# Column sums of w_out in another PSUM bank, its loads ordered ahead, and two pairs with unsplit attention weights

## The chip, the cores and the metric

One of the eight cores of a Trainium2 chip runs the whole program. The metric is the device time of one execution in microseconds; the kernel before takes 1210.42 us (median of three runs, 1209.32 to 1211.03). A core has five engines that each work through their own list of instructions in order and wait for each other by semaphores: PE (TensorE, matrix products, with PEld for its weight loads), DVE (VectorE), ACT (ScalarE), POOL (GpSimd) and SP (SyncE, which here issues every DMA). Matrix products land in PSUM, eight banks of 128 x 512 float32 values.

## The reference

Attention with a sigmoid in place of a softmax, followed by a two-layer feed-forward net with an ELU between the layers. Eight batches, twelve heads, 448 positions, head size 64; model width 768, hidden width 2048. `moe_w_in` and `moe_w_out` are float64.

```python
scores = scale * np.matmul(q, k.transpose(0, 1, 3, 2)) - np.log(S)
attn = 1.0 / (1.0 + np.exp(-scores))
x = np.matmul(attn, v)                  # (8, 12, 448, 64) -> 3584 tokens x 768
h = x @ w_in                            # 768 -> 2048
g = np.where(h > 0.0, h, np.exp(np.minimum(h, 0.0)) - 1.0)
out = g @ w_out                         # 2048 -> 768
```

## The kernel before

**Numbers in two halves.** To keep precision at float16 speed, a float32 operand is scaled by a power of two and split into a high and a low float16 part (`split`: ACT writes the high part, DVE the low one from it). A product of two split operands is three matmuls: high x high, low x high, high x low. The scales come from the largest value of an operand, or, for the two weights, from the sum of magnitudes down a column.

**Order of the work.** The heads of a batch go in six pairs. Batch 0 (`b < EXACT`) is done with unsplit float32 operands: scores, sigmoid, then values against the float32 attention weights, while the tiles of `w_in` are loaded, decoded from float64 and split beside it. Then `hidden(0, w_out_beside)` runs the first layer of batch 0 (`moe1`, sixteen tiles `ph` of 18 matmuls), with the work on `w_out` beside it. From batch 1 on, each batch's six pairs are interleaved with the second layer (`moe2`, tiles `po`) of the batch ahead, and its own first layer follows.

**w_out.** `load_w_out` takes its two column halves i = 0 and 1, each in sixteen row tiles f. For each tile there is a load of 384 KB, two ACT passes (`magnitudes`, L154 and L158), a DVE pass (L159), one matmul of the magnitudes against ones into the PSUM tile `so` (L166), and a DVE pass that puts the sign back (`signed`, L173). When all sixteen are summed, `sum_magnitude` (L180 to L182) makes the scale, and sixteen splits (L137 on ACT, L138 on DVE) write the two halves into `wo`. The split of tile f writes over the place of magnitudes f-2, so ACT's split waits for DVE's split two tiles back. The generator is advanced by `step`: four pieces per `ph` tile from the third on, and what is left in the first pairs of batch 1 (`step(3 if hp < NC - 1 else NF)`). The raw tiles have no buffers of their own: they lie in parts of `wo` that are not yet written (eight places for half 0, two for half 1) or in the three buffers with the tag "at", so a load waits for `signed` of the tile whose place it takes.

**PSUM.** Three buffers have the tag "pm" (the `ph` and `po` tiles, small sums, and `so`), two of two banks have "psc" (scores), one has "pav" (a pair's sum over values; `ph` tile 3 of each batch also uses it).

**A pair from batch 1 on.** `prepare` finds the scales (DVE's `mx`, a matmul `pr`, small DVE and POOL steps), splits q and k (`nat`), sends them through a transposing DMA into `qk`, and splits the values into `vn`. `Pair.scores` makes three score tiles `psc0` to `psc2` of two heads, and one (`pscr`) for the last keys of two pairs; `soften` is the sigmoid on ACT (L400, into `sg`); `Pair.parts` splits `sg` into `at` (L436 on ACT, L437 on DVE) and the last keys into `ar` (L425, L427); `Pair.values` multiplies these by `vn` into `pav`; `finish` splits `pav` into `xh`.

**What sets the order.** Up to the end of batch 0's first layer a scheduler places each engine's instructions, DMAs on SP among them; the loop over batches 1 to 7 stands in the order in which it is written (`manual_schedule`), and leftovers of the first part are merged between its instructions. So a change in the first part can move any instruction there.

Of the kernel before, what the change touches and what calls it, by code (L numbers as in the profile page):

```python
# [34 lines left out]
def attention_ffn(  # L35
# [22 lines left out]
    WR, WT = 5, 5  # L58
    EXACT = 1
    SP = 4  # L60
    SKEW = 2
    W_IN = [1, 3, 6, 9, 12, 15, 16]
    W_LOAD = [1, 1]
    W_OUT = 4
    assert 2 * D == P and 2 * R == P and NK == NP

# [151 lines left out]
    def load_w_out(wo):  # L218


        for i in range(NH):
# [5 lines left out]
            ]  # L227
            sums = ps.tile([P, 512], F32, tag="pm", name=f"so{i}", bufs=3)
            for f in range(NF):

                if i == 0 and f >= 2:
                    st = wo[:, 1, f % 8 * 2 :][:, :2]
                elif i == 1 and f % 2 and f < NF - SP - SKEW:
                    st = wo[:, 1, NF - SP + f // 2 % 2 * 2 :][:, :2]
                else:
                    st = None
# [7 lines left out]
                )  # L244
                lo, hi, hl = words(st)
                t = whole[f].unsqueeze(1)
# [30 lines left out]

    def load_v(b, hp):
        rv = rvs[(b * NP + hp) % len(rvs)]
        both = slice(2 * hp, 2 * hp + 2)  # L280
# [10 lines left out]
    def value_scale(b, hp, pv, c, xs):  # L291
# [7 lines left out]
        nc.vector.reciprocal(vi[:, hp : hp + 1], vm[:, hp : hp + 1])  # L299
        if b < EXACT:  # L300
            nc.gpsimd.tensor_scalar(c, vi[:, hp : hp + 1], 2.0 ** (XTOP - XBITS), None, op0=ALU.mult)
# [6 lines left out]
    def prepare(b, hp, raw, rv, xs):  # L308
# [34 lines left out]
        def transposed(sc):  # L343
# [23 lines left out]
            parts = [qk[:, i].rearrange("p t x -> p (t x)") for i in range(2)]  # L367

            vn = sb.tile([P, 2, 2 * NC + 2, D], F16, tag="vn", name=f"vn{u}", bufs=3)
            split(vn[:, 0], vn[:, 1], rv, sc[:, 0:1])  # L370
# [4 lines left out]
    class Pair:  # L375
# [42 lines left out]
        def parts(self, g):  # L418

            if g == NC:  # L420
                (sg, i) = self.sg[g]
# [20 lines left out]
        def values(self, g):  # L442
            if g == 0:
                self.pav = ps.tile([P, 512], F32, tag="pav", name=f"pav{self.u}")
            pav, sg, vv = self.pav, self.sg.pop(g), self.vs
            if g == NC and self.b < EXACT:
                for j, r in enumerate(rows):
                    nc.tensor.matmul(
                        pav[r, :S], vv[0][r, 2 * NC + j], sg[0][r, 0], start=False, stop=True
                    )  # L450
# [78 lines left out]
    def moe1(b, g, xh, m, first, beside=None):  # L529
# [8 lines left out]
        for f in range(NF):  # L538

            if f == 3:  # L540
                ph = ps.tile([P, 512], F32, tag="pav", name=f"ph{b}_{f}")
# [126 lines left out]
    def w_out_beside(f):  # L668
        nonlocal wo, steps
        if f == 0:  # L670
            w_in_ratios()
            wo = sb.tile([P, NH, NF, 2, HM], F16, tag="wo", name="wo")
            steps = load_w_out(wo)
        if f >= 2:
            step(W_OUT)
# [172 lines left out]
```

## Time and profile before

| | before |
|---|---|
| median of three runs | 1210.42 us |
| profiled execution | 1210.77 us |
| span of its instructions | 1209.0 us |
| PE busy | 1153.2 us (95%) |
| DVE busy | 827.7 us (68%) |
| ACT busy | 719.3 us (59%) |
| POOL busy | 103.0 us (9%) |
| granted PE clock over the span | 0.982 |
| read from and written to memory | 59.77 MB and 11.01 MB |

The span is counted from the first to the last instruction; the execution's own time is 1.8 us longer. The shares are means over stages with different limits, so a stage has to be read by itself. "Idle before" in a row is the time for which the engine stood just before that instruction, with the instruction or transfer that ended it.

### The profile page before, as it was taken

The page shows a single profiled execution, that of the slowest core. Times are in us where ns is not written, and L with a number is a line of the kernel's source. Part 1 is how long each engine was busy: PE and PEld are TensorE (multiplying, and loading weights), DVE is VectorE, ACT ScalarE, POOL GpSimd, SP SyncE. Part 2 cuts the span into 40 slices and gives each one's busy share as a digit, 9 for nine tenths or more (in the row PEclk, how much of TensorE's full clock was granted, in tenths as well). Part 3 has the DMA queues.
Part 4 walks back from the last instruction along what each step waited for, and adds up shares of the span by engine and source line. Part 5 has one row for each costly group of instructions (what it writes and reads, how often), then busy time and mean ns, then how long its engine had stood idle before and what let it go on. Part 6 is the DMA issues. An engine that isn't in the chain of part 4 may idle for free.

```text
span 1209.0 us, 24046 instructions
## 1 busy us (share of the span) xinstructions
PE 1153.2 (95%) x9674; PEld 639.0 (53%) x9674; DVE 827.7 (68%) x1742; ACT 719.3 (59%) x1099; POOL 103.0 (9%) x275
## 2 busy tenths in 40 slices
PE   6879785999999999999999999999999999999998
PEld 2324343555566555655566555655566555555565
DVE  5797888977667675977667666886667666865500
ACT  4875788864666446864666446864566446863300
POOL 1021001200011000200011000200011000100000
PEclk9999897999999999999999999999999999999999
DMA  8955632441124212441124212441124211310000
GB/s 224 279 145 117 210 104 74 93 99 40 40 60 93 60 40 47 93 100 40 40 60 93 60 40 47 85 107 40 40 54 99 60 40 40 76 29 8 1 27 27
DMA packets 219568, 91.62 MB, mean 76 GB/s; under 512 B 183616, under 2 KB 215360, under 8 KB 219456
## 3 DMA queue, kind: packets, MB, share of 16 engines
q1 hardware_dynamic: 219456, 90.09, 30.9%
q8 instruction: 75, 1.23, 0.4%
q14 instruction: 37, 0.30, 0.1%
HBM read 59.77 MB, written 11.01 MB: 59 GB/s over the span
## 4 chain that ended last, share of the span: by engine, by line
PE 83%; DVE 6%; ACT 4%; DMA 3%; SPq 2%; issue 1%; POOL 0%; DVEq 0%; ACTq 0%
PE ph L549 32%; PE po L581 30%; PE pav L459 7%; PE psc L392 7%; PE po_r L581 5%; PE pscr L479 1%; DMA stage<-in_moe_w_in_dram 1%; SPq L269 1%; DMA wo<-in_moe_w_out_dram 1%; DVE mx L141 1%; DVE wo L138 1%; DVE stage L159 1%; ACT wo L154 1%; DVE wi L138 1%; ACT wo L158 0%
## 5 line engine op out<-in xcount | busy, mean ns | idle before, releaser
L549 PE MATMUL ph<-xh,wi 128*128 128x448 f16 x2304 | 446.9, 356 | 12.7 <-DVE xh L500 5.1
L581 PE MATMUL po<-wo,g 128*64 128x384 f16 (+1 forms) x4320 | 395.0, 329 | 1.9 <-DVE alw L180 1.7
L581 PEld LDWEIGHTS <-g 128*64 128x64 f16 (+1 forms) x4992 | 290.8, 109 | 164.3 <-issue 33.1
L549 PEld LDWEIGHTS <-wi 128*128 128x128 f16 x2304 | 225.1, 99 | 230.2 <-issue 22.3
L437 DVE SCALAR_TENSOR_TENSOR at<-sg,at 128x896 f16<-128x896 f32 x126 | 134.0, 1090 | 91.5 <-ACT at L436 91.3
L561 ACT ACTIVATE e<-ph,msc 128x448 f32<-128x448 f32 x128 | 80.9, 633 | 185.7 <-PE ph L549 160.7
L400 ACT ACTIVATE sg<-psc,bias,sc 128x896 f32<-128x896 f32 x126 | 133.8, 1094 | 3.8 <-PE psc L392 0.5
L563 DVE TENSOR_SCALAR e<-e 128x448 f32<-128x448 f32 x128 | 50.2, 393 | 117.3 <-ACT e L561 117.2
L436 ACT ACTIVATE at<-sg 128x896 f16<-128x896 f32 x126 | 114.9, 947 | 0.7
L137 ACT ACTIVATE g<-e,msc 128x384 f16<-128x384 f32 (+1 forms) x192 | 96.2, 533 | 9.9 <-DVE e L564 8.5
L137 ACT ACTIVATE xh<-pav,sc 128x448 f16<-128x448 f32 x48 | 30.4, 633 | 116.3 <-PE pav L459 114.8
L138 DVE SCALAR_TENSOR_TENSOR g<-e,msc,g 128x384 f16<-128x384 f32 (+1 forms) x192 | 94.7, 522 | 2.4 <-ACT g L137 1.9
L392 PE MATMUL psc<-qk 64*128 64x448 f16 x756 | 87.2, 353 | 4.8 <-ACT sg L400 4.8
L564 DVE SCALAR_TENSOR_TENSOR e<-ph,msc,e 128x448 f32<-128x448 f32 x128 | 87.4, 683 | 4.1
L459 PE MATMUL pav<-at,vn 128*64 128x448 f16 x756 | 79.3, 355 | 0.0
L459 PEld LDWEIGHTS <-vn 128*64 128x64 f16 x924 | 53.1, 111 | 33.0
L137 ACT ACTIVATE nat<-raw,sc 128x384 f16<-128x384 f32 (+1 forms) x126 | 60.9, 535 | 13.5 <-POOL sc L334 9.1
L336 POOL TENSOR_SCALAR sc<-pw 128x1 f32<-128x1 f32 x42 | 12.0, 286 | 640.8 <-DVE pw L103 537.5
L581 PE MATMUL po_r<-wo,g 128*64 128x384 f16 (+1 forms) x672 | 64.9, 326 | 0.0
L138 DVE SCALAR_TENSOR_TENSOR nat<-raw,sc,nat 128x384 f16<-128x384 f32 (+1 forms) x126 | 60.8, 526 | 3.4 <-ACT nat L137 1.1
L392 PEld LDWEIGHTS <-qk 64*128 64x128 f16 x756 | 30.2, 94 | 53.4 <-issue 34.6
L589 DVE TENSOR_SCALAR o<-po,osc 128x384 f32<-128x384 f32 x48 | 29.4, 612 | 41.1 <-PE po L581 36.4
(108 smaller groups left out, 936.7 us busy)
## 6 DMA issues: line engine op xcount, KB each, us to landing
stage<-in_moe_w_in_dram SPq DMA_DIRECT2D x16, 768.0 KB, 6.3
raw<-in_q_dram SPq DMA_DIRECT2D x96, 96.0 KB, 3.3
raw<-in_k_dram SPq DMA_DIRECT2D x96, 96.0 KB, 2.8
rv<-in_v_dram SPq DMA_DIRECT2D x48, 192.0 KB, 2.8
out_dram<-o SPq DMA_DIRECT2D x48, 192.0 KB, 2.1
wo<-in_moe_w_out_dram SPq DMA_DIRECT2D x19, 384.0 KB, 4.1
so<-in_moe_w_out_dram SPq DMA_DIRECT2D x13, 384.0 KB, 4.1
rv<-in_v_dram SPq DMA_DIRECT2D x96, 32.0 KB, 2.5
```

What stands on the lines that cost most here:

```text
L137: nc.scalar.mul(hi, src, s)
L138: nc.vector.scalar_tensor_tensor(lo, src, s, hi, op0=ALU.mult, op1=ALU.subtract)
L392: nc.tensor.matmul(psc[:, j, :S] if g < NC else psc[rows[j], 0, :S], kk[rows[j], o], qq[rows[j], :S], start=(n == 0), stop=(n == len(parts ...
L400: a = nc.scalar.activation(to, psc, AF.Sigmoid, bias=bias, scale=self.s_scale)
L436: nc.scalar.mul(hi, sg, 2.0**ATOP)
L437: nc.vector.scalar_tensor_tensor(lo, sg, 2.0**ATOP, hi, op0=ALU.mult, op1=ALU.subtract)
L459: nc.tensor.matmul(pav[rows[j], :S], vv[i][:, 2 * NC + j if g == NC else j * NC + g], sg[k][:, j], start=(g == 0 and n == 0), stop=(g == N ...
L549: nc.tensor.matmul(ph[:, :S], wi[:, wj, c, f * P : (f + 1) * P], xh[:, c, xj], start=(n == 0), stop=(n == 3 * NK - 1),)
L561: a = nc.scalar.activation(e, ph[:, :S], AF.Exp, scale=inv)
L563: nc.vector.tensor_scalar(e, e, 1.0, -1.0, op0=ALU.min, op1=ALU.add)
L564: nc.vector.scalar_tensor_tensor(e, ph[:, :S], inv, e, op0=ALU.mult, op1=ALU.max)
L581: nc.tensor.matmul(po[r, :HM], tokens[:, r], wo[:, i, f, wj], start=(n == 0), stop=(n == 3 * NF - 1),)
```

## The change

1. The sums of `w_out` (`so`) take the PSUM buffer "pav" in place of one of the three "pm" buffers. In batch 0's first layer, tile 3 no longer takes "pav".
2. `load_w_out` issues its loads ahead of their use: six tiles ahead for half 0 and two for half 1 (`W_AHEAD`), and its first piece is stepped at f = 0 (`step(1)`).
3. For the first two pairs of batch 1 (`WHOLE = EXACT * NP + 2`), `parts` returns at once: the attention weights stay in `sg` as float32, the values are loaded a second time as float32 into `vw` (one load of 192 KB and two of 32 KB for a pair) in place of the split into `vn`, and `values` multiplies the two unsplit. The scale of the result follows in `value_scale`.

```diff
+    WHOLE = EXACT * NP + 2
...
+    W_AHEAD = [6, 2]
...
-            sums = ps.tile([P, 512], F32, tag="pm", name=f"so{i}", bufs=3)
-            for f in range(NF):
-
+            sums = ps.tile([P, 512], F32, tag="pav", name=f"so{i}")
+            loads = []
+
+            def load(f):
+                if f >= NF:
+                    return
                 if i == 0 and f >= 2:
                     st = wo[:, 1, f % 8 * 2 :][:, :2]
                 elif i == 1 and f % 2 and f < NF - SP - SKEW:
...
+                loads.append(st)
+
+            early = W_AHEAD[i]
+            for f in range(early):
+                load(f)
+            for f in range(NF):
+                load(f + early)
+                lo, hi, hl = words(loads[f])
                 t = whole[f].unsqueeze(1)
                 magnitudes(t, lo, hi, hl, sums[:, :HM], f == 0, f == NF - 1)
...
-    def load_v(b, hp):
-        rv = rvs[(b * NP + hp) % len(rvs)]
+    def load_v(b, hp, rv=None):
+        if rv is None:
+            rv = rvs[(b * NP + hp) % len(rvs)]
...
-        if b < EXACT:
+        if b * NP + hp < WHOLE:
             nc.gpsimd.tensor_scalar(c, vi[:, hp : hp + 1], 2.0 ** (XTOP - XBITS), None, op0=ALU.mult)
...
+            if b * NP + hp < WHOLE:
+                whole = sb.tile([P, 2 * NC + 2, D], F32, tag="vn", name=f"vw{u}", bufs=3)
+                return x_scale, s_scale, parts, [load_v(b, hp, whole)]
...
         def parts(self, g):
 
+            if len(self.vs) == 1:
+                return
...
-            if g == NC and self.b < EXACT:
-                for j, r in enumerate(rows):
+            if g == NC and len(vv) == 1:
+                i = sg[1] if len(sg) > 1 else 0
+                for j in range(2):
+                    r = rows[j ^ i]
                     nc.tensor.matmul(
-                        pav[r, :S], vv[0][r, 2 * NC + j], sg[0][r, 0], start=False, stop=True
+                        pav[rows[j], :S], vv[0][r, 2 * NC + j], sg[0][r, i],
+                        start=False, stop=True,
                     )
                 return
...
-            if f == 3:
+            if f == 3 and b >= EXACT:
                 ph = ps.tile([P, 512], F32, tag="pav", name=f"ph{b}_{f}")
...
             steps = load_w_out(wo)
+            step(1)
```

Three places show how instructions move; line numbers of the changed kernel are those of its own text (L159 is L161 there, L173 is L175, L138 is L140, L242 is L247, L437 is gone for these pairs).

DVE, from the last sums of w_out's half 1 to the splits that follow them, before (`so_13` to `so_15` are raw tiles, `at_0` the split weights of pair 0 of batch 1, `nat_2` and `vn_2` pair 2's split q, k and values, `mx_3` pair 3's maxima, `swo` the scales of w_out):

```order
L159 SCALAR_TENSOR_TENSOR to_1_1357<-to_1_1357,so_15_1532 128x384
L437 SCALAR_TENSOR_TENSOR at_0_1640<-sg_0_1636,at_0_1640 128x896
L173 SCALAR_TENSOR_TENSOR to_1_1357<-so_15_1532,to_1_1357 128x384
L180 TENSOR_REDUCE alw<-so_1358 128x1
L437 SCALAR_TENSOR_TENSOR at_0_1643<-sg_0_1638,at_0_1643 128x896
...
L437 SCALAR_TENSOR_TENSOR at_0_1754<-sg_0_1750,at_0_1754 128x896
L427 SCALAR_TENSOR_TENSOR ar_0_1757<-sgr_0_1749,ar_0_1757 64x448 x2
L138 SCALAR_TENSOR_TENSOR wo<-wo,swo_1568 128x384 x2
...
L138 SCALAR_TENSOR_TENSOR vn_2_1771<-rv_85,sc_2_1708,vn_2_1771 128x512
L141 TENSOR_REDUCE mx_3_1784<-rv_86 128x4
L141 TENSOR_REDUCE mx_3_1784<-raw_3_906 128x7
```

and in the change:

```order
L140 SCALAR_TENSOR_TENSOR vn_2_1761<-rv_85,sc_2_1706,vn_2_1761 128x512
L143 TENSOR_REDUCE mx_3_1774<-rv_86 128x4
L143 TENSOR_REDUCE mx_3_1774<-raw_3_908 128x7
L161 SCALAR_TENSOR_TENSOR wo<-wo,so_13_1486 128x384
L161 SCALAR_TENSOR_TENSOR to_0_1333<-to_0_1333,so_14_1493 128x384
...
L161 SCALAR_TENSOR_TENSOR to_1_1334<-to_1_1334,so_15_1524 128x384
L175 SCALAR_TENSOR_TENSOR to_0_1333<-so_14_1493,to_0_1333 128x384
L175 SCALAR_TENSOR_TENSOR to_1_1334<-so_15_1524,to_1_1334 128x384
L182 TENSOR_REDUCE alw<-so_1335 128x1
...
L140 SCALAR_TENSOR_TENSOR wo<-wo,swo_1545 128x384 x13
```

Pair 2's splits and pair 3's maxima now stand ahead of the last three sums, the `at` and `ar` of pair 0 are gone, and thirteen splits of w_out follow the scale in one piece.

PE at the same place, before:

```order
L166 MATMUL so_1358<-wo,ones 128x384
...
L166 MATMUL so_1358<-to_0_1356,ones 128x384
...
L166 MATMUL so_1358<-to_1_1357,ones 128x384
L581 LDWEIGHTS g
L581 MATMUL po_1_0_1828<-wo,g 64x384
...
L459 LDWEIGHTS vn_0_806
L459 MATMUL pav_0_1841<-at_0_1640,vn_0_806 64x448
```

and in the change:

```order
L602 MATMUL po_1_0_1818<-wo,g 64x384
...
L168 MATMUL so_1335<-to_1_1334,ones 128x384
L480 MATMUL pav_0_1831<-sg_0_1640,vw_0_806 64x448 x2
L480 MATMUL pav_0_1831<-sg_0_1642,vw_0_806 64x448 x2
L480 MATMUL pav_0_1831<-sg_0_1748,vw_0_806 64x448 x2
L468 MATMUL pav_0_1831<-sgr_0_1747,vw_0_806 64x448 x2
```

The piece of `po` that stood between the last sum and pair 0's values (twelve matmuls) now stands ahead of the last sums, and `pav` follows them at once, in the bank that the sums leave.

SP, the loads of w_out behind pair 1's transposing DMA, before (`qk_0`, `qk_1` are pairs 0 and 1, `raw_3` and `rv_86` pair 3's inputs):

```order
L364 DMA_TRANSPOSE qk_0_804<-nat_0_797 128x14x128
...
L364 DMA_TRANSPOSE qk_1_891<-nat_1_884 128x14x128
...
L273 DMA raw_3_906<-in_k_dram 64x2x64
L281 DMA rv_86<-in_v_dram 128x2x192
L286 DMA rv_86<-in_v_dram 64x2x64 x2
L242 DMA wo<-in_moe_w_out_dram 128x384 x8
```

and in the change:

```order
L247 DMA wo<-in_moe_w_out_dram 128x384
L377 DMA_TRANSPOSE qk_0_804<-nat_0_797 128x14x128
...
L377 DMA_TRANSPOSE qk_1_892<-nat_1_885 128x14x128
...
L285 DMA raw_3_908<-in_k_dram 64x2x64
L247 DMA wo<-in_moe_w_out_dram 128x384 x8
```

One load of w_out now stands ahead of both transposing DMAs and pair 3's value loads have moved ahead of them; the other loads still follow pair 3's inputs. Earlier on SP, in batch 0, the six loads of `vw` are added and two raw tiles of w_out move behind the next tiles of w_in.

More of the change, by code (lines that the diff above doesn't have):

```diff
@@ L244, in load_w_out @@
                 )
-                lo, hi, hl = words(st)
+                loads.append(st)
[5 more added lines that the diff above has]
+                lo, hi, hl = words(loads[f])
                 t = whole[f].unsqueeze(1)
```

## The prediction, made before the changed kernel had run

> **What bounds the kernel now.** I first cut the span into stages by the busy time of each engine (columns: stage, its length, then busy us and instructions of PE, PEld, DVE, ACT and POOL, granted clock, DMA share, GB/s).
>
> ```profile
> 0.00:84.00 84.00, 63.47 (x324) 25.03 (x324) 62.58 (x155) 61.15 (x78) 9.74 (x26) 0.94 0.85 230
> 84.00:206.00 122.00, 92.73 (x546) 45.96 (x546) 103.20 (x232) 84.85 (x154) 12.22 (x31) 0.87 0.43 126
> 206.00:232.00 26.00, 24.39 (x268) 14.26 (x266) 22.20 (x44) 22.92 (x34) 5.16 (x10) 0.95 0.38 74
> 232.00:1209.00 977.00, 972.58 (x8545) 553.76 (x8541) 639.68 (x1314) 550.42 (x836) 75.85 (x209) 1.00 0.25 56
> ```
>
> From 232 us on PE is busy for 972.58 of 977 us: there only PE work counts, and the change touches none of it. From 84 to 206 us (first layer of batch 0, w_out, first pair of batch 1) PE stands for 29.3 us while DVE works 103.2 of 122. So whatever lets PE leave this stage sooner shortens the span one for one, and the question is what DVE and its suppliers gain. Next the waits of PE and of DVE there (waiter, releaser, us in total, times, longest).
>
> ```profile
> PE ph L549 <- DVE xh L500: 5.1, 1, 5.1
> PE so L166 <- DVE wo L159: 4.4, 5, 2.0
> PE ph L549 <- DVE alw L180: 3.8, 1, 3.8
> PE psc L392 <- ACT sg L400: 3.8, 1, 3.8
> PE pr L129 <- DVE mx L319: 3.7, 1, 3.7
> DVE wo L159 <- ACT wo L158: 7.6, 5, 3.1
> DVE wo L159 <- ACT so L158: 4.5, 3, 3.1
> ```
>
> Nearly all of PE's waits end on DVE, the last big one on ACT's sigmoid. DVE itself waits 12.1 us for the two ACT passes over raw w_out tiles, which in turn wait for loads. The timeline of 186 to 207 us shows how PE's last stall is made:
>
> ```profile
> 186.08 0.48 PE L166 MATMUL so<-to,ones 128*128 128x384 bf16 x1 [1.12 <-DVE to L159]
> 186.14 1.09 DVE L437 SCALAR_TENSOR_TENSOR at<-sg,at 128x896 f16<-128x896 f32 x1
> 187.62 0.55 DVE L180 TENSOR_REDUCE alw<-so 128x1 f32<-128x384 f32 x1
> 189.16 0.14 DVE L181 TENSOR_SCALAR alw<-alw 128x1 f32<-128x1 f32 x1
> 189.83 0.23 DVE L253 TENSOR_SCALAR swo<-wn,swo 128x16 f32<-128x16 f32 x1
> 191.16 1.27 DVE L427 SCALAR_TENSOR_TENSOR ar<-sgr,ar 64x448 f16<-64x448 f32 x2
> 194.31 1.65 PE L581 MATMUL po<-wo,g 128*64 128x384 f16 x18
> 194.54 1.62 DVE L138 SCALAR_TENSOR_TENSOR nat<-raw,sc,nat 128x384 f16<-128x384 f32 x3 [0.93 <-ACT nat L137]
> 196.16 0.75 DVE L138 SCALAR_TENSOR_TENSOR vn<-rv,sc,vn 128x512 f16<-128x512 f32 x1
> 197.42 1.08 DVE L141 TENSOR_REDUCE mx<-raw 128x7 bf16<-128x896 f32 x1
> 199.71 2.45 DVE L138 SCALAR_TENSOR_TENSOR wo<-wo,swo 128x384 f16<-128x384 f32 x4
> 204.01 0.61 ACT L137 ACTIVATE xh<-pav,sc 128x448 f16<-128x448 f32 x1
> 204.53 2.08 ACT L400 ACTIVATE sg<-psc,bias,sc 128x896 f32<-128x896 f32 x2
> 205.66 1.30 PE L392 MATMUL psc<-qk 64*128 64x448 f16 x6 [3.80 <-ACT sg L400]
> ```
>
> The last sum of w_out's half 1 is at 186.08. After it come `at` and `ar` of pair 0, twelve splits of w_out with `nat`, `vn` and `mx` between them, `xh`, the sigmoid of pair 1, and only then can PE take pair 1's third scores, at 205.66: 19.6 us after the last sum. Past that PE has small stalls only. I use this point as the finish line.
>
> **The change part by part.** The sum is made against the profiled execution (1210.77 us, span 1209.0; 1.8 us lie around the span), which is 0.35 us above the median of 1210.42.
>
> *From the last sum to the finish line.* In the change's order nothing of pair 0 and no `nat`, `vn` or `mx` is left there. What stays: two sign passes and the maximum after the matmul (186.08 to 188.17 with an `at` among them; without it about 1.5), the short steps to `swo` (189.16 to 190.06, 0.9), thirteen splits, `xh` (0.5 from its start to the next start on ACT) and one sigmoid (half of 2.08). The splits run ACT, DVE, ACT in turn because of the place they overwrite: four take 2.45 + 0.15 on DVE, 0.65 each, so thirteen take 8.4. Sum 1.5 + 0.9 + 8.4 + 0.5 + 1.0 = 12.3 in place of 19.6: **-7.3**. PE's own chain in that time is shorter and is no bound: 2 for the bank, 3.7 for the values (below), 1.3 for the first two score tiles (six matmuls alone took that in the last row above, with the clock low), then 18 and 12 matmuls of `po` at 1.65 for 18, 2.8: 9.8 in all.
>
> *When the last sum comes.* The moved group (`nat`, `vn`, two `mx`: 194.54 to 198.5, 4.0) now stands ahead of the last three tiles. Before, DVE and ACT stood there until those tiles' loads came, and the group fills that hole:
>
> ```profile
> 182.04 0.55 ACT L154 ACTIVATE wo<-so 128x384 f32<-128x384 f32 x1 [4.33 <-DMA so<-in_moe_w_out_dram]
> 183.06 0.56 DVE L159 SCALAR_TENSOR_TENSOR wo<-wo,so 128x384 uint32<-128x384 uint32 x1 [3.09 <-ACT so L158]
> 102.93 0.74 DVE L138 SCALAR_TENSOR_TENSOR vn<-rv,sc,vn 128x512 f16<-128x512 f32 x1
> ```
>
> With DVE's 3.1 of idle time filled it costs +0.9. The two `vn` splits at 98 and 103 us vanish, 0.74 each: -1.5.
>
> *The loads.* The first tiles of w_out reach ACT late, and DVE behind it; the second group of loads is paced by the places they go to.
>
> ```profile
> 115.17 5.68 SPq L242 DMA_DIRECT2D wo<-in_moe_w_out_dram x8
> 118.69 0.55 ACT L154 ACTIVATE wo<-wo 128x384 f32<-128x384 f32 x1 [3.20 <-DMA wo<-in_moe_w_out_dram]
> 119.72 0.56 DVE L159 SCALAR_TENSOR_TENSOR wo<-wo 128x384 uint32<-128x384 uint32 x1 [3.08 <-ACT wo L158]
> SPq L242 <- DVE wo L173: 38.3, 10, 10.0
> ```
>
> In the change one load goes ahead of the transposing DMAs and the rest start after pair 3's q and k, some 2 us sooner, the three value loads of 1.9 us having moved up. DVE's five waits of this kind are 7.6 us in all, and that is the one bound; the other is 0, if ACT's new place for the early tile makes it wait there instead. I take -2, by how much sooner the loads start. The 38.3 us that SP waits for sign passes stay: the places are the same, so "ahead" beyond eight tiles is only on paper. I give it nothing.
>
> *The bank.* The 3.8 us wait of `ph` for the maximum of the sums goes, as `ph` has all three "pm" buffers. PE then stands elsewhere, since DVE sets the pace here: bounds 0 and -3.8, taken 0.
>
> *PE's extra work.* Float32 values take two records for each product:
>
> ```profile
> 67.06 1.83 PE L459 MATMUL pav<-sg,rv 128*64 128x448 f32 x8 [0.60 <-DVE xh L138]
> 62.35 0.97 PE L448 MATMUL pav<-sg,rv 64*64 64x448 f32 x4
> 212.68 1.87 PE L459 MATMUL pav<-at,vn 128*64 128x448 f16 x18
> 214.38 0.54 PE L459 MATMUL pav<-ar,vn 128*64 128x448 f16 x4
> 219.72 0.74 PE L392 MATMUL psc<-qk 64*128 64x448 f16 x6 [0.96 <-ACT sg L400]
> ```
>
> Two steps take 1.83, so a pair takes 3 x 0.91 + 0.97 = 3.7, against 2.2 for the split one (212.68 to 214.86): +1.5 a pair. For pair 0 it lies within the 12.3 us. For pair 1 it counts, but pair 1's `at` and `ar` leave ACT and DVE (4.5 us of DVE), and so the stalls of 0.96 and, with the releases around it, about 1.6 in all from 206 to 232 (26 - 24.4). Net -0.1.
>
> [...]
>
> *Batch 0.* Six loads are added to SP while it issues without a pause:
>
> ```profile
> 41.39 1.33 SPq L286 DMA_DIRECT2D rv<-in_v_dram x2
> 47.58 2.89 SPq L281 DMA_DIRECT2D rv<-in_v_dram x1
> 51.95 0.90 ACT L154 ACTIVATE stage<-stage 128x768 f32<-128x768 f32 x1 [2.21 <-DMA stage<-in_moe_w_in_dram]
> ```
>
> A pair's value loads hold SP for some 1.9 us (0.5 and 1.4), two pairs 3.8. Part of it falls into the wait at 47.58, and two raw w_out tiles move behind; but ACT waits for w_in just after. Bounds 0 and +3.8, taken +1.
>
> Sum: -7.3 + 0.9 - 1.5 - 2 - 0.1 + 1 = -9.0. Span 1200.0, execution 1201.8, median 1201.4.
>
> **The rivals.**
>
> *Only the removed work counts.* The waits for places move but don't shrink, so DVE is done sooner by what it no longer does up to the finish line: two `vn`, three `at` of 1.09 and `ar` of 1.27, 6.0 in all, less 0.65 for the thirteenth split; with +1 from batch 0 and -0.1 it is -4.5: 1206. For it speak the 38.3 us; against it that the group fills a hole which is there.
>
> *All of DVE's waits for w_out go.* The 12.1 us come on top of 6.0 - 0.65, less batch 0's +1: about -16.5, 1194. For it: every wait of this kind is a lateness of a few us. Against it: the places.
>
> *The change doesn't do what it says.* Seven of the first eight loads stay behind pair 3's inputs in SP's order, so the run ahead is one tile. If SP's 3.8 us then come through in full in place of +1, the removed work's -4.5 shrinks to -1.7, within the noise: 1209.
>
> *Slower: the values wait for the bank.* PE takes instructions in order, and `pav` of pair 0 now stands right behind the last sum, in its bank; behind it stand pair 1's scores, for which ACT and DVE wait. The finish line is 12.3 us after the last sum, so the change is slower from the point at which that sum comes later than 205.66 - 12.3 = 193.4, 7.3 later than now. It would take ACT's `nat` of pair 2 (which waits for pair 2's scales from PE and POOL) to hold back the last raw tiles. With the sum at 197 the time is 1214. Against it: the idle 4.33 of ACT that the group can use.
>
> **How the numbers follow.** Forecast 0.45; only removed work 0.20; all waits 0.16; no effect 0.08; slower 0.11. About 0.2% (2.4 us) is what a measurement can tell from no change. The first three are faster: 0.81; same 0.08; slower 0.11. The predicted time is the forecast's 1201.4, its own range 1197 to 1205 (the bounds of the loads and of batch 0). The range takes in the second case, most of the third and of no effect, and leaves out the slower one: 1193.5 to 1209.5.
>
> **What would show it.** PE's wait for `alw` ahead of `ph` is gone; from the last sum to the first third-scores of pair 1 it is about 12 us, with a wait of some 2 us on `sg`; that point is at about 196; no ACT wait over 2 us at the last three raw tiles; pair 0's values take 3.7 us on PE; DVE's idle time from 84 us to that point is down from about 19 us to about 13. The prediction is wrong if the last sum comes after 188, if the first 84 us get longer by more than 2, or if PE has new waits after 232.

## The result, and the profile after

The change takes 1202.49 us (median of 4 runs, 1201.61 to 1203.07) against 1210.41 (4 runs, 1209.32 to 1211.03) for the kernel before in the same session: ratio 0.9936, 95% interval 0.9921 to 0.9952. Its profiled execution has a span of 1199.8 us, 9.2 less than before. The forecast was 1201.4 us and a span of 1200.0. The profiled execution is the fastest of the four; by the medians the gain is 7.9 us. So the number held, but of its terms several did not, and they cancelled: that it came so close is luck. The experiments are about that.

The stages of the change, from 84 us to the finish line (TensorE's third scores of pair 1) and from there to 250 us (columns: stage, its length, busy us and instructions of PE, PEld, DVE, ACT and POOL, granted clock, DMA share, GB/s):

```profile
0.00:84.00 84.00, 59.13 (x308) 23.29 (x308) 58.71 (x144) 58.86 (x76) 7.00 (x24) 0.97 0.88 236
84.00:199.02 115.02, 92.77 (x551) 44.27 (x552) 101.07 (x237) 81.75 (x150) 11.66 (x32) 0.92 0.46 133
199.02:250.00 50.98, 50.98 (x570) 29.34 (x571) 42.39 (x85) 41.41 (x58) 6.67 (x21) 1.00 0.48 102
```

and the same of before, cut at its own finish line:

```profile
84.00:205.66 121.66, 92.40 (x543) 45.82 (x542) 102.86 (x231) 84.51 (x154) 12.22 (x31) 0.87 0.44 126
205.66:250.00 44.34, 42.73 (x478) 25.24 (x479) 38.93 (x77) 38.41 (x54) 10.34 (x21) 0.97 0.45 94
```

The finish line moved from 205.66 to 199.02, 6.64 us. DVE does 1.8 us less up to there and stands idle for 13.95 us in place of 18.8. Behind the line PE is busy for every microsecond (50.98 of 50.98) at full clock; before it lost 1.61 us there and ran at 0.97. From the finish line to the end of the span it was 1003.3 us and is 1000.8: another 2.6 us. In the first 84 us PE and DVE have done about 4 us less work than before (59.13 against 63.47, 58.71 against 62.58), and ACT 2.3 us less.

The timeline of TensorE in the change from the last sum of w_out on (start, length, instruction, and in brackets the idle time before it and what ended it):

```profile
186.56 0.48 PE L168 MATMUL so<-to,ones 128*128 128x384 bf16 x1 [1.48 <-DVE to L161]
188.16 3.90 PE L480 MATMUL pav<-sg,vw 128*64 128x448 f32 x12 [1.12 <-DVE alw L182]
191.99 0.97 PE L468 MATMUL pav<-sgr,vw 64*64 64x448 f32 x4
199.02 0.74 PE L408 MATMUL psc<-qk 64*128 64x448 f16 x6 [2.23 <-ACT sg L416]
199.69 5.07 PE L602 MATMUL po<-wo,g 128*64 128x384 f16 x60
204.59 2.42 PE L480 MATMUL pav<-sg,vw 128*64 128x448 f32 x12
206.95 0.97 PE L468 MATMUL pav<-sgr,vw 64*64 64x448 f32 x4
```

From the last sum to the finish line it is 12.46 us (19.58 before), with 2.23 of waiting for the sigmoid; the bank makes the values wait 1.12. The six scores and sixty `po` at the finish line take 0.74 and 5.07 where they took 1.30 and 5.95 before: the same matmuls, 1.44 us faster.

The waits of PE and of DVE from 84 to 206 us, and then SyncE's queue (SPq) in the timeline, at the float32 value loads and at the second group of w_out loads:

```profile
PE pav L480 <- DVE xh L140: 5.3, 1, 5.3
PE so L168 <- DVE wo L161: 4.6, 3, 4.0
DVE wo L161 <- ACT wo L160: 4.8, 5, 2.7
DVE wo L161 <- ACT so L160: 1.6, 1, 1.6
DVE to L161 <- ACT so L160: 1.3, 2, 0.9
```

```profile
37.72 0.59 SPq L294 DMA_DIRECT2D vw<-in_v_dram  x1
38.36 1.64 SPq L299 DMA_DIRECT2D vw<-in_v_dram  x2
40.05 0.59 SPq L294 DMA_DIRECT2D vw<-in_v_dram  x1
40.69 1.24 SPq L299 DMA_DIRECT2D vw<-in_v_dram  x2
42.03 0.54 SPq L294 DMA_DIRECT2D rv<-in_v_dram  x1
118.23 4.08 SPq L247 DMA_DIRECT2D wo<-in_moe_w_out_dram  x8
```

No `ph` waits for `alw` any more. DVE's waits for raw w_out tiles went from 12.1 to 6.4 us (with the last two tiles, `to`, from 12.5 to 7.7), though the second group of loads starts later than before, at 118.23 in place of 115.17. The six float32 loads hold SyncE from 37.72 to 41.93 us, and the next value load is issued at 42.03 instead of 39.61.

### The profile page after: what moved, and what is told of

It is laid out like the page before. It is cut to its first block, busy times and chain, and to the rows that moved or that the text cites. A ratio compares the mean times of both kernels' runs of the same rounds, so it can differ in the third digit from the quotient of the medians.

```text
span 1199.8 us, 24004 instructions
## 1 busy us (share of the span) xinstructions
PE 1148.5 (96%) x9662; PEld 634.7 (53%) x9662; DVE 817.2 (68%) x1730; ACT 710.1 (59%) x1087; POOL 95.9 (8%) x275
## 4 chain that ended last, share of the span: by engine, by line
PE 85%; DMA 5%; DVE 4%; ACT 3%; SPq 2%; issue 1%; DVEq 0%; POOL 0%; ACTq 0%; POOLq 0%
PE ph L570 32%; PE po L602 31%; PE pav L480 7%; PE psc L408 7%; PE po_r L602 5%; DMA stage<-in_moe_w_in_dram 3%; PE pscr L500 1%; DMA wo<-in_moe_w_out_dram 1%; SPq L281 1%; ACT sg L416 1%; DMA so<-in_moe_w_out_dram 1%; ACT wo L139 1%; DVE wo L175 1%; DVE wo L140 1%; DVE wi L140 1%
## 5 line engine op out<-in xcount | busy, mean ns | idle before, releaser
L570 PE MATMUL ph<-xh,wi 128*128 128x448 f16 x2304 | 441.7, 353 | 1.7 <-DVE e L585 0.9
L455 DVE SCALAR_TENSOR_TENSOR at<-sg,at 128x896 f16<-128x896 f32 x120 | 127.6, 1091 | 92.2 <-ACT at L454 92.2
L454 ACT ACTIVATE at<-sg 128x896 f16<-128x896 f32 x120 | 109.4, 947 | 0.6
L140 DVE SCALAR_TENSOR_TENSOR g<-e,msc,g 128x384 f16<-128x384 f32 (+1 forms) x192 | 94.8, 522 | 1.9 <-ACT g L139 1.5
L480 PE MATMUL pav<-at,vn 128*64 128x448 f16 x720 | 74.8, 353 | 0.0
L480 PEld LDWEIGHTS <-vn 128*64 128x64 f16 x880 | 49.9, 110 | 31.2
L140 DVE SCALAR_TENSOR_TENSOR nat<-raw,sc,nat 128x384 f16<-128x384 f32 (+1 forms) x126 | 60.6, 526 | 3.9 <-ACT nat L139 1.8
L140 DVE SCALAR_TENSOR_TENSOR xh<-pav,sc,xh 128x448 f16<-128x448 f32 x48 | 32.6, 680 | 37.1 <-ACT xh L139 37.1
```

Of the source, the lines that this page charges most:

```text
L140: nc.vector.scalar_tensor_tensor(lo, src, s, hi, op0=ALU.mult, op1=ALU.subtract)
L454: nc.scalar.mul(hi, sg, 2.0**ATOP)
L455: nc.vector.scalar_tensor_tensor(lo, sg, 2.0**ATOP, hi, op0=ALU.mult, op1=ALU.subtract)
L480: nc.tensor.matmul(pav[rows[j], :S], vv[i][:, 2 * NC + j if g == NC else j * NC + g], sg[k][:, j], start=(g == 0 and n == 0), stop=(g == N ...
L570: nc.tensor.matmul(ph[:, :S], wi[:, wj, c, f * P : (f + 1) * P], xh[:, c, xj], start=(n == 0), stop=(n == 3 * NK - 1),)
```

## The experiments

All twelve stand beside runs of the kernel before on the same chip; ratios are to it. The ratios come from 5 to 11 runs of a kernel (the change's from 4); the other columns, in us, come from its one profiled execution, and executions of one kernel differ by 1 to 4 us. Differences of less than a microsecond between two rows are not more than hints. Where the last two sums stand in one row, the start of the last one is that row's end less 0.48.

| kernel | ratio (95%) | last sum | to the finish line | finish line | from there to the end |
|---|---|---|---|---|---|
| before | 1 | 186.08 | 19.58 | 205.66 | 1003.3 |
| the change | 0.9936 (0.9921-0.9952) | 186.56 | 12.46 | 199.02 | 1000.8 |
| values_only | 0.9986 (0.9977-0.9994) | 192.54 | 11.51 | 204.05 | 1002.5 |
| bank_loads | 1.0004 (0.9995-1.0013) | 184.06 | 20.96 | 205.02 | 1003.7 |
| values_bank | 0.9931 (0.9918-0.9945) | 187.27 | 11.63 | 198.90 | 1000.8 |
| late_loads | 0.9931 (0.9918-0.9943) | 185.59 | 12.47 | 198.06 | 1000.8 |
| values_order | 0.9973 (0.9963-0.9983) | 191.96 | 11.63 | 203.59 | 1000.8 |
| one_pair | 0.9933 (0.9921-0.9946) | 183.78 | 12.74 | 196.52 | 1003.3 |
| three_pairs | 0.9955 (0.9941-0.9968) | 186.82 | 12.46 | 199.28 | 1002.1 |
| late_fourth | 0.9924 (0.9911-0.9936) | 186.46 | 12.45 | 198.91 | 1000.8 |
| group_behind | 0.9953 (0.9940-0.9965) | 189.84 | 11.64 | 201.48 | 1000.8 |
| late_second | 0.9979 (0.9970-0.9988) | 189.93 | 12.46 | 202.39 | 1000.8 |
| late_front | 0.9921 (0.9909-0.9934) | 184.65 | 12.73 | 197.38 | 1000.8 |
| second_front | 0.9957 (0.9943-0.9971) | 188.25 | 12.74 | 200.99 | 1000.8 |

Three things are read off the columns. Between the last sum and the finish line it is 11.5 to 12.7 us wherever pair 0 is unsplit, and 20 to 21 where it is split. Behind the line it is 1000.8 us wherever two pairs are unsplit and PE comes to the line with its clock up (granted 1.00 from the line to 250 us in the change; in values_only 0.96, and 1002.5 us). So what is left to tell kernels apart is when the last sum comes, and that ranges over 9 us.

### Which of the three edits

**values_only**: the kernel before with the unsplit pairs alone.

```diff
-            sums = ps.tile([P, 512], F32, tag="pav", name=f"so{i}")
+            sums = ps.tile([P, 512], F32, tag="pm", name=f"so{i}", bufs=3)
...
-            if f == 3 and b >= EXACT:
+            if f == 3:
...
-    W_AHEAD = [6, 2]
+    W_AHEAD = [0, 0]
...
-            step(1)
```

> The kernel before with the unsplit weights and float32 values of pairs 0 and 1 alone: the sums stay in a bank of their three, the loads are not issued ahead. Theory (the time between the last sum and the finish line is shortened by what the pairs no longer do there, and the other two edits add little): last sum to finish line about 12 us as in the change (12.46 there, 19.6 before), batch 0 as slow as in the change (last split of w_in on VectorE ending at about 103.4 us, 99.6 before), and the time the change's plus the 2 us that the prediction gave to the loads: 1204.5 us. Rival 1 (bank and loads are worth nothing): 1202.5, the change's own time. Rival 2 (the gain came from the bank and the loads): 1209 to 1214.

1207.44 us, ratio 0.9986: a quarter of the gain, and none of the three numbers named ahead had it. The stretch behind the last sum shrank as expected (11.51), but the last sum came 6 us later than in the change. TensorE's timeline in this kernel:

```profile
185.96 0.33 PE L168 MATMUL so<-wo,ones 128*128 128x384 bf16 x1 [1.80 <-DVE wo L161]
186.57 2.58 PE L480 MATMUL pav<-sg,vw 128*64 128x448 f32 x12
191.99 0.34 PE L168 MATMUL so<-to,ones 128*128 128x384 bf16 x1
192.54 0.34 PE L168 MATMUL so<-to,ones 128*128 128x384 bf16 x1
204.05 1.30 PE L408 MATMUL psc<-qk 64*128 64x448 f16 x6 [8.85 <-ACT sg L416]
```

Without the shared bank nothing holds pair 0's values back, and they stand ahead of the last two sums; PE then has little left and waits 8.85 us at the line.

**bank_loads**: the change with `WHOLE = EXACT * NP`.

```diff
-    WHOLE = EXACT * NP + 2
+    WHOLE = EXACT * NP
```

> The change with both pairs split as before: only the bank and the loads that run ahead are left. Theory: last sum to finish line stays near 19.6 us, the first 84 us are those of before (VectorE's last split of w_in ends at 99.6 us), and the loads give what the prediction gave them, 2 us: 1208.4 us. Rival 1 (bank and loads are worth nothing): 1210.4. Rival 2 (they are the gain): 1203 or less.

1209.75 us, ratio 1.0004: the bank and the run ahead are worth nothing measurable by themselves (rival 1). So neither the values alone nor the bank alone make the gain; together they do.

**values_bank**: the change without the run ahead.

```diff
-    W_AHEAD = [6, 2]
+    W_AHEAD = [0, 0]
...
-            step(1)
```

> The change without the run ahead of the loads and without the early first step. By the prediction's term for the loads it is 2 us slower than the change: 1204.5 us, with waits of VectorE for raw w_out tiles from 84 us to the finish line up from 7.7 us to about 10 to 12. If the loads ahead are worth nothing: 1202.5. If the loads were the whole cut of VectorE's waits (12.5 to 7.7 us): 1207.

1201.04 us, ratio 0.9931 against the change's 0.9936, and finish lines of 198.90 and 199.02: the run ahead is worth nothing that these runs can tell. DVE's waits for raw tiles (4.7, 1.6 and 1.0 us) are not longer than the change's.

### What the bank brings

**values_order**: values_only, with pair 0's first values put behind the last sum in TensorE's written order (the bank as before).

```diff
+                    if self.b == EXACT and self.hp == 0 and g == 0:
+                        tc.add_manual_dep(mm.ins, last_sum[0], ...)
```

> The first experiment (unsplit weights and float32 values alone, sums in a bank of the three as before) with one thing more: on TensorE pair 0's values are put behind the last sum of w_out in the written order. In the first experiment they stood ahead of the last two sums, which came at 191.99 and 192.54 us, 6 us later than in the change, and the finish line followed 11.5 us later at 204.05. Theory (the shared bank does nothing but force this order): last sum at 186 to 188 us, finish line at 198.5 to 200, time that of the change without the run ahead, 1201.0 us. Rival (the bank matters by itself, since the sums hold one of the three first-layer buffers): the time stays near 1207.4, or falls by less than 2.

1206.27 us, ratio 0.9973: 1.2 us of the 6.4 between values_only and values_bank. The theory that the bank forces PE's order and nothing else fell. By the profiles even this part is hardly the last sum, which comes 0.58 sooner, and the line 0.46: the stage behind the line is 1.6 us shorter, as PE waits 1.88 us at the line in place of 8.85 and keeps its clock (granted 1.00 from the line to 250 us in place of 0.96; the scores and the sixty `po` take 0.74 and 5.07 in place of 1.30 and 6.11). PE now waits for the last raw tiles, which ACT and DVE reach late. The timelines of ACT (three rows) and PE (two) in this kernel:

```profile
184.10 0.54 ACT L156 ACTIVATE wo<-so 128x384 f32<-128x384 f32 x1 [2.77 <-DMA so<-in_moe_w_out_dram]
186.19 1.40 ACT L139 ACTIVATE nat<-raw,sc 128x384 f16<-128x384 f32 x3
188.11 0.55 ACT L156 ACTIVATE to<-so 128x384 f32<-128x384 f32 x1
167.92 3.56 PE L578 MATMUL ph<-xh,wi 128*128 128x448 f16 x18
191.49 0.95 PE L168 MATMUL so<-to,ones 128*128 128x384 bf16 x2 [4.84 <-DVE to L161]
```

The group of pair 2's `nat`, `vn` and pair 3's maxima, which in the change stands ahead of tile 13 while its load is under way, stands behind it here: first ACT waits 2.77 us, then it works on the group.

**group_behind**: values_bank with the group behind raw tile 13 in ACT's written order.

```diff
-        nc.scalar.mul(hi, src, s)
+        a = nc.scalar.mul(hi, src, s)
+        if after:
+            tc.add_manual_dep(a.ins, after, ...)
...
+                    passes[-3] if b == EXACT and hp == 2 else None,
```

> The change without the run ahead (1201.0 us), with one thing more: pair 2's nat splits, and with them vn and pair 3's maxima, are put behind raw tile 13 of w_out in the written order of ScalarE; VectorE's order from there on is then that of the experiment in which only TensorE's order was changed (1206.3 us), and the two differ in the bank. In that one the group stood between tiles 13 and 14: ScalarE waited 2.77 us for tile 13's load, then worked 4 us on the group with tiles 14 and 15 already there, and the last sum came at 191.5 us. Theory (what the bank brought is the group's place in the hole that waits for tile 13; the bank itself brings little): last sum at 190.5 to 192, time 1205 to 1206.5. Rival (the buffers themselves: the first layer's last tile starts at 153 us with the shared bank and at 168 without it): the last sum stays at 187 to 188.5, time 1201 to 1202.

1203.62 us, ratio 0.9953, last sum at 189.84: between the two. Against values_bank, which has the same bank, the group's place costs 2.6 us; against values_order, which has the same place, the shared bank is worth 2.65. ACT waits at tile 13 as in values_order, but the first layer is done 14 us sooner. The timelines of PE and ACT:

```profile
153.80 3.38 PE L581 MATMUL ph<-xh,wi 128*128 128x448 f16 x17
183.21 0.54 ACT L164 ACTIVATE wo<-so 128x384 f32<-128x384 f32 x1 [3.37 <-DMA so<-in_moe_w_out_dram]
184.09 1.40 ACT L139 ACTIVATE nat<-raw,sc 128x384 f16<-128x384 f32 x3
189.37 0.95 PE L178 MATMUL so<-to,ones 128*128 128x384 bf16 x2 [4.07 <-DVE to L171]
```

So the 6.4 us of the bank are three parts: PE's order 1.2, the group's place 2.6, and 2.65 that come with the three buffers for the first layer. The kernels ran on three chips, each beside runs of the kernel before, and the intervals of neighbouring ratios overlap a little, so a part is known to about a microsecond; the finish lines give 0.46, 2.58 and 2.11. For the last part the traces show the earlier first layer (its last tile at 153.80 against 167.92) and that its waits on `alw` (2.9) and on `e` (5.9) are gone or small; which piece of that sets the last sum was not tried apart.

### Batch 0

**late_loads**: the change with the six float32 value loads behind the last load of w_in on SyncE.

```diff
-                return x_scale, s_scale, parts, [load_v(b, hp, whole)]
+                late.append((b, hp, whole))
+                return x_scale, s_scale, parts, [whole]
...
+    for b_hp_rv in late:
+        load_v(*b_hp_rv, last_load[0])
```

> The change with the six float32 value loads placed behind the last load of w_in in SyncE's order (at about 75 us, where its queue has long gaps) in place of 38 to 42 us; the same loads, the same bytes. Theory (batch 0 is slower by some 4 us in the change because these loads hold SyncE and push the next value and w_in loads behind them): VectorE's last split of w_in ends at about 99.6 us as before, and the time falls by nearly 4 us, to 1198.5 to 1199.5. Rival (batch 0 is slower for another reason, such as the order of the engines, or the lost time is made up by the wait for w_out tiles behind it): 1202 to 1203.

1200.89 us, ratio 0.9931 against the change's 0.9936: in the ratio the rival's number (the time lies between the two forecasts), though the theory's first half held. The loads left at 69.0 us, and DVE's work in the first 84 us was 64.36 us, as much as before and more. But the finish line came only 0.96 sooner. The time was lost again at the last raw tiles, as the timelines of DVE, SyncE and ACT show:

```profile
175.78 1.02 DVE L175 SCALAR_TENSOR_TENSOR wo<-so,wo 128x384 uint32<-128x384 uint32 x2
176.71 0.75 DVE L140 SCALAR_TENSOR_TENSOR vn<-rv,sc,vn 128x512 f16<-128x512 f32 x1
177.97 0.55 DVE L175 SCALAR_TENSOR_TENSOR wo<-so,wo 128x384 uint32<-128x384 uint32 x1
175.89 1.57 SPq L389 DMA_TRANSPOSE qk<-nat  x1
177.91 1.62 SPq L249 DMA_DIRECT2D so<-in_moe_w_out_dram  x3
181.63 0.54 ACT L156 ACTIVATE wo<-so 128x384 f32<-128x384 f32 x1 [5.88 <-DMA so<-in_moe_w_out_dram]
```

Tiles 13 to 15 wait for the places that the sign passes of tiles 10 to 12 free (L175), and on SyncE for the transposing DMA ahead of them; ACT then stands 5.88 us for tile 13.

**late_second**: the same for pair 1's three loads alone.

```diff
-                late.append((b, hp, whole))
+                if hp:
+                    late.append((b, hp, whole))
+                else:
+                    load_v(b, hp, whole)
```

> The change with pair 1's three float32 value loads behind the last load of w_in on SyncE, and pair 0's left where they are. With pair 1 split (three early loads fewer) the last sum came at 183.8 us and the finish line at 196.5, 2.5 us sooner than in the change; the stage behind it then lost this again. Theory (the three loads more in batch 0 cost those 2.5 us, and pair 1's unsplit work is worth 2.3 us behind the finish line): finish line at 196 to 197, time 1199.5 to 1200.3. Rival (the last sum is set by the order that comes out, not by those loads): last sum at 185 to 187, time 1201 to 1202.5.

1206.56 us, ratio 0.9979: worse than the change by 4 to 5 us, and the theory that three loads cost 2.5 us fell. Here the written order put the whole group ahead of the sign passes of tiles 10 to 12; the loads followed, and ACT stood 7.41 us (timelines of DVE and ACT):

```profile
179.84 1.08 DVE L143 TENSOR_REDUCE mx<-raw 128x7 bf16<-128x896 f32 x1
180.83 1.49 DVE L175 SCALAR_TENSOR_TENSOR wo<-so,wo 128x384 uint32<-128x384 uint32 x3
185.96 0.54 ACT L156 ACTIVATE wo<-so 128x384 f32<-128x384 f32 x1 [7.41 <-DMA so<-in_moe_w_out_dram]
```

**late_fourth**: late_loads with a fourth place for raw tiles of half 1, three loads ahead for that half, and pair 2's transposing DMA behind the last load of w_out.

```diff
+                if i == 1 and f in (6, 12):
+                    st = sb.tile([P, 1, HM], U64, tag="rw", name=f"so{i}_{f}")
...
-    W_AHEAD = [6, 2]
+    W_AHEAD = [6, 3]
```

> The fourth experiment (the float32 value loads behind the last load of w_in) with a fourth place for raw tiles of w_out's half 1 (tiles 6 and 12 go there, so tiles 13 to 15 find their places one tile sooner), three loads ahead for half 1, and pair 2's transposing DMA behind the last load of w_out on SyncE. In the fourth experiment ScalarE stood 5.88 us for tile 13, whose load was issued at 177.9 us behind that DMA. Theory (places and SyncE's order set when the last sum comes): that wait falls under 2 us, the last sum comes at 182 to 183 us in place of 185.59, the time falls by 3 us to about 1198. Rival (VectorE's and ScalarE's amount of work sets it): 1200.5 to 1201.5, no change.

1200.34 us, ratio 0.9924: a miss. The order changed with the place: the sign passes of tiles 10 to 13 moved to 179.4 and later, and ACT stood 6.13 us for tile 14. A place is no gain if the pass that frees it is written late.

**late_front** and **second_front**: late_loads and late_second with one stretch in another order, the group behind the sign passes of tiles 10 to 12 on VectorE and the transposing DMA behind the last loads on SyncE. Nothing is removed or added.

```diff
+                    signs[-4] if b == EXACT and hp == 2 else None,
...
+            if b == EXACT and hp == 2:
+                behind(d, last_out[0], "behind the last load of w_out")
```

> The fourth experiment (float32 value loads behind the last load of w_in, 1200.9 us) with one stretch written in another order: on VectorE pair 2's nat, vn and pair 3's maxima stand behind the sign passes of raw tiles 10 to 12, which free the places of tiles 13 to 15, and on SyncE pair 2's transposing DMA stands behind the last loads of w_out. ScalarE's order is the same. Theory (the last sum comes when tiles 13 to 15 arrive, and these wait for those sign passes and for SyncE; the group fills the hole only if it stands between the two): sign passes of 10 and 11 at about 175 us in place of 175.78, of 12 at 176 in place of 177.97, loads from 175.5 in place of 177.91, last sum at about 183.3 in place of 185.59, time 1198.6 us. Rival (the last sum is bound by VectorE's and ScalarE's work): 1200.5 to 1201.5.

> The experiment with pair 1's value loads alone moved (1206.6 us; there the group stood ahead of the sign passes of tiles 10 to 12, these came at 180.83 us, the loads of tiles 13 to 15 at 182.18, ScalarE stood 7.41 us for them and the last sum came at 189.93) with the same reordering as in the run beside it. Theory: sign passes from 177.8, loads from about 178.5, last sum at about 186.5 to 187, time 1203 to 1203.5 us or, with the group's 4 us wholly in the hole, down to 1201. Rival: the time stays at 1206 or above.

1199.38 us (0.9921) and 1203.94 us (0.9957). The last sum came 0.94 and 1.68 sooner than in the kernel without the reordering, the finish lines 0.68 and 1.40: the direction held in both, the last sum moved by about half of what was expected, and the intervals of the ratios with and without the reordering still touch. In late_front's timeline (DVE, ACT, PE) the three sign passes stand together, and the group fills part of the hole:

```profile
176.41 1.50 DVE L187 SCALAR_TENSOR_TENSOR wo<-so,wo 128x384 uint32<-128x384 uint32 x3 [0.50 <-PE so L179]
177.82 1.41 DVE L149 SCALAR_TENSOR_TENSOR nat<-raw,sc,nat 128x384 f16<-128x384 f32 x3
180.45 0.55 ACT L167 ACTIVATE wo<-so 128x384 f32<-128x384 f32 x1 [3.75 <-DMA so<-in_moe_w_out_dram]
184.65 0.48 PE L179 MATMUL so<-to,ones 128*128 128x384 bf16 x1 [0.54 <-DVE to L172]
```

The passes came 1.4 us later than expected, 0.50 of it a wait for PE's sums. late_front has the lowest time of all kernels here. Its interval overlaps the change's, so that it beats the kernel before is shown (ratio 0.9921) and that it beats the change is not.

### How many pairs

**one_pair** and **three_pairs**: `WHOLE = EXACT * NP + 1` and `+ 3`.

```diff
-    WHOLE = EXACT * NP + 2
+    WHOLE = EXACT * NP + 1
```

> The change with pair 0 alone unsplit; pair 1 of batch 1 is split again. The prediction gave pair 1 a net of -0.1 us (float32 values on TensorE against at and ar on VectorE and ScalarE). If that is right: 1202.6 us, the change's time. If the stalls after the finish line are VectorE's and ScalarE's work on pair 1 (from the finish line to the third scores of pair 2, 27.24 us before and 24.93 in the change, of which 1.44 is the slower clock after the wait): 1.0 to 1.5 us slower than the change, 1203.5 to 1204. If float32 values cost TensorE their full 1.0 us there (3.39 against 2.41): 1201.5.

> The change with pair 2 unsplit as well, with three more float32 value loads. From the third scores of pair 1 on TensorE hardly waits in the change, so its 1.0 us more for a float32 pair counts in full and what VectorE saves does not, while pair 2's vn split (0.74 us) no longer stands ahead of the last sums: 1203 us. Rival (VectorE's work still counts in that stage): 1201 or less. Three more early loads in batch 0 could add up to 2 us to either.

one_pair: 1201.60 us, ratio 0.9933, the change's within the intervals, as the prediction had it. But the net of nothing is made of two large parts: with pair 1 split the finish line comes at 196.52, 2.5 sooner, and the stage behind it takes 1003.3 in place of 1000.8, 2.5 longer, as PE waits 0.72, 1.48 and 0.24 there, and smaller pieces. three_pairs: 1204.23 us, ratio 0.9955, and a span 1.6 us longer than the change's. Behind the finish line, where PE hardly waits, the third float32 pair adds 1.3 us (1002.1 against 1000.8), of which the values are 1.0: 2.42 and 0.97 in place of 1.87 and 0.55. The finish line itself (199.28) shows no gain from the missing `vn`; whether the three loads more in batch 0 took it back was not tried apart.

## Why the prediction was right or wrong

- **What bounds the kernel**: right. PE from the finish line on, and one microsecond at the line is one in the time: in eight of the experiments, and in the change, the rest takes 1000.8 us.
- **From the last sum to the finish line, 12.3**: right, 12.46, and 11.5 to 12.7 in the eleven experiments with pair 0 unsplit; the PE wait of some 2 us on `sg` measured 2.23.
- **When the last sum comes, -1.6 (group +0.9, `vn` -1.5, loads -2, batch 0 +1)**: wrong; it came 0.48 later. The loads' -2 is the step that failed: "by how much sooner the loads start" took the start from the written order, and the loads start 3 us later (118.23); taking the run ahead out changes nothing (values_bank). The group did fill the hole (ACT's wait at tile 13 fell from 4.33 to 1.42 us), but the hole was a matter of order, and it is worth 2.6 us only where the group stands behind the sign passes that free the places and ahead of tile 13 (group_behind, late_second). The `vn` term was not measured apart.
- **Batch 0, +1 within 0 to +3.8**: the number came out at the finish line (late_loads takes 0.96 back), by luck: it is too small in the first 84 us, where PE and DVE are some 4 us behind. The prediction's own sign of failure, a first stage longer by more than 2, was met there and did not matter, because the last raw tiles wait for places and, as late_loads suggests, the loss falls into that.
- **The bank, 0 within 0 to -3.8**: wrong as a term of a sum. By itself it is 0 (bank_loads), with the unsplit values 6.4 us, outside the bounds; some 1.6 us of that is PE's clock behind the line. The step that failed is "PE then stands elsewhere, since DVE sets the pace here": once `at` and `ar` are gone, the group's place and the three buffers for the first layer bring the last sum forward, by 2.57 and 2.12 us in the profiles, and PE's own order by 0.58. The rival that spoke of the bank had the sign wrong: that pair 0's values wait for the last sum cost 1.12 us, and without it they went ahead of the sums.
- **Pair 1, -0.1**: right as a net (one_pair), wrong in what stands behind the finish line, where the change saves 2.6 us. 1.44 of it is PE's clock, which the prediction did not count: it read the 1.30 us of the six scores as their cost "with the clock low" and not as something that the change gives back. The rest is mostly PE's stalls, which cover 4.2 us behind the line in place of 6.0, less 0.98 for the float32 values.
- **Float32 values, 3.7 a pair**: 3.39 for pair 1 at full clock, 4.87 for pair 0, whose first 2.9 us ran at a granted clock of 0.50; pair 0's lay under the thirteen splits as said. The prediction's 3.7 is added up from the lengths of rows, while the 2.2 beside it goes from start to start (212.68 to 214.86); from start to start pair 1's took 3.26 in the change (204.59 to 207.85). And batch 0 was no like stretch: pairs of float32 records started 0.43 us apart there and 0.375 apart in the change, both at a granted clock of 1.00. Why they were slower stays open.
- **The sum**: -9.0 expected, -9.2 in the span of the profiled execution, -7.9 in the medians. The last sum is 2.1 us later than expected, the stage behind the line 2.5 us shorter; 12.3 against 12.46 is the part that was understood. Of the rivals, "the change doesn't do what it says" was right about the loads, and it was no reason for a small gain. DVE's idle time up to the line fell to 13.95 us (13 expected); the line came at 199.02 and not at 196.

## What to carry to other kernels

A buffer that is shared can help by the order that it forces (of the 6.4 us here 1.2 are PE's order and 2.6 the group's place): add up edits only after asking which of them the others need, and time the pairs of edits as well as each alone. Between the pass that frees a place and the consumer of the load that takes it lay a hole of some microseconds here (4.33 us of waiting in ACT at tile 13 before). Work put ahead of the freeing passes delayed the load (late_second, 7.41), work put behind the consumer left most of the hole empty (group_behind, 3.37), and only work between the two filled it, mostly or in part (1.42 left in the change, 3.75 in late_front). Read the granted clock in stretches of a quarter of a microsecond around every long wait of PE, and count what a lower clock costs in the matmuls behind it as part of the wait's price (1.44 us at the finish line here).

## What the runs showed of the hardware that was not expected

The clock did not go by the length of the last wait alone. In the three kernels in which PE stood 3.80 us (before), 4.63 (bank_loads) and 8.85 (values_only) ahead of the finish line, the six score matmuls took 1.30 us; in the eleven in which it stood 0.83 to 2.28 us they took 0.74. In the kernel before, the sixty `po` behind them took 5.95 us and in the change 5.07; together 1.44 us. But in before and bank_loads the clock had fallen already, in the wait of 3.71 and 3.64 us for pair 3's maxima (`mx`) a little earlier, so that the twelve `po` ahead of the line took 2.16 us in place of the change's 1.15. In the change those maxima stand ahead of tile 13, and that wait is gone. And in the change a wait of 4.00 us ends in a matmul at full clock (0.33), while the next one, after 0.68, is slow (0.48). The timeline of PE in before (three rows) and in the change (three):

```profile
199.68 0.22 PE L129 MATMUL pr<-mx,ones 128*64 128x12 bf16 x2 [3.71 <-DVE mx L319]
199.71 2.16 PE L581 MATMUL po<-wo,g 128*64 128x384 f16 x12
206.90 5.95 PE L581 MATMUL po<-wo,g 128*64 128x384 f16 x60
183.60 0.33 PE L168 MATMUL so<-wo,ones 128*128 128x384 bf16 x1 [4.00 <-DVE wo L161]
184.61 0.48 PE L168 MATMUL so<-to,ones 128*128 128x384 bf16 x1 [0.68 <-DVE to L161]
195.65 1.15 PE L602 MATMUL po<-wo,g 128*64 128x384 f16 x12
```

Read in stretches of a quarter of a microsecond, the granted clock is 1.00 or 0.50 except where it changes, and from 20 to 230 us each change, in the profiles of before and of the change, lies a whole multiple of 3.41 us behind the one before it: among them those at 184.83, 191.66, 198.49 and 208.72 in before and at 184.25 and 191.07 in the change. So the steps of the one lie some 0.6 us from those of the other. The busy time of PE (first figure behind the length) in single steps and the clock in them (third figure from the end): a step of before and one of values_only behind which the clock falls, and the two steps of the change around its wait at the line, behind which it stays:

```profile
195.08:198.49 3.41, 0.89 (x12) 0.47 (x9) 3.29 (x7) 2.05 (x4) 0.00 (x0) 1.00 0.35 68
193.81:197.22 3.41, 1.21 (x15) 0.82 (x14) 2.44 (x8) 2.20 (x4) 2.19 (x6) 1.00 0.49 118
194.49:197.90 3.41, 2.30 (x30) 1.48 (x27) 2.90 (x6) 3.04 (x7) 0.00 (x0) 1.00 0.02 5
197.90:201.31 3.41, 2.29 (x26) 1.38 (x27) 2.65 (x10) 3.37 (x5) 0.79 (x4) 1.00 0.16 58
```

The steps behind which the clock fell were not wholly idle: PE worked 0.89 us in the one of before, and 1.21 us in the one of values_only, which ended 2.0 us into the wait. Behind the two of the change, with 2.30 and 2.29 us of work, it stayed at 1.00. At what share of work it falls, no run here shows.

The place of one group of DVE and ACT work of about 4 us, with no instruction added or removed, moved the last sum by 1 to 3 us (0.94 in late_front, 1.68 in second_front, 2.57 in group_behind), and small edits in batch 0 moved that group, since the order of that stretch is laid out anew with each edit.
